# Output projection: its weights and first operands made beside the last segment's projections, in tiles taken over from them

## The chip, the cores and the metric

One core of one Trainium2 chip. The metric is the device time of one execution in microseconds (us). The engines are PE (TensorE, matmuls), DVE (VectorE), ACT (ScalarE), POOL (GpSimd) and SP (SyncE, which issues most DMAs); each runs its own instructions in order.

## What is computed

A transformer block on x of 2048 rows and 512 columns, in fp32. The reference, cut to what matters:

```python
mod = (silu(c) @ w_mod).reshape(1, 6, 1, 512)          # sa, ca, ga, sb, cb, gb
h = layernorm(x) * (1 + ca) + sa
# attention in N = 4 segments of 512 rows, 32 heads of 16
q, k, v = h @ wq, h @ wk, h @ wv
for s in range(4):
    p = softmax(q_s k_s^T / 4 + mask)                  # mask: -1e9 where query index < key index
    a_mem = phi(q_s) M / (phi(q_s) z + 1e-6)
    o_s = g * a_mem + (1 - g) * (p @ v_s)
    M, z = M + phi(k_s)^T v_s, z + sum(phi(k_s))
x = x + ga * (o @ wo)                                  # the output projection
h = layernorm(x) * (1 + cb) + sb
x = x + gb * (((h @ w_gate) * (h @ w_up)) @ w_down)    # 1376 features
```

## The kernel before, in words

**fp32 by three products.** An operand a of the projections is kept as a high part aH (fp32r, a copy by ACT) and a low part aL = a - aH (a subtraction by DVE or POOL). A product is then three matmuls: high x high, low x high, high x low.

**Stages.** At the start, the modulation and the projections of segment 0. Then the attention loop (line 1088), passes v from -2 to 32, for 32 units u of four heads each (eight units a segment). Pass v, in five slots, makes the maxima of units v+1 and v+2 (`q_step`: logits on PE, masked maximum on DVE), the exponentials of unit v (`k_step`: logits on PE, Exp on ACT, masking on POOL), and the sums p @ v of unit v-1 (`av_step`, slot 1: 32 matmuls into "tb", line 353). Behind the loop come the rest of segment 3's output projection and the GLU (lines 1272 to 1451).

**Work beside the attention.** Other PE work is written as generators that yield a cost after each small group of matmuls. In each slot `fill` (line 1019) adds a quarter of the rate (5.2 from pass 20 on, so 1.3 a slot; slot 1 adds nothing) to a credit and takes steps of the generators until the credit is used: first `fill_a`, and when that has ended `fill_b`. A step that yields 0.0 takes no credit, `False` ends the slot, and `None` says that nothing can be done yet. `weave(a, b, at)` takes steps of b behind those steps of a whose number stands in `at`. `pin` orders an instruction behind the PE instruction issued last.

- `fill_a` (line 932): K and Q projections of the four head groups of each segment (`a_kq`: 12 matmuls into "kps" or "qps", a yield of 0.68 after each three), V (`a_v`), the layer norm of the next segment, the memory sums (`a_mem`, `a_memT`). In the last segment, s = 3, it goes K, Q of group 0, V, K, Q of groups 1 and 2, then Q and K of group 3. Behind V it loads the attention output of segment 0 (`wo_load`, tiles "orl") and the first two of four row blocks of wo (`wo_raw`, tiles "wor"), which POOL scales by ga (line 916).
- `fill_b` (line 988): `open_b` closes the projections' pool `pa` and opens `bc` and `pb` in its place, allocates the output projection's weights woH and woL there, loads and scales row blocks 2 and 3 of wo, and splits all four into woH (ACT, line 928) and woL (POOL and DVE, line 929). Beside it `wo_op(0)` splits the operands of segment 0 into oH (ACT, line 487) and oL (DVE, line 490, in place). The first four of these steps yield `False`, one a slot (`paced`). Then `wo_mm(0)`: for each of four row tiles t, four steps of three matmuls into "wops" (line 517), a yield of 0.68 after each, and then `wo_add`, which adds x (tile "xr", loaded by `xr_load`) on DVE and stores the row tile. Woven into it are the rest of the operands, the first tile of the GLU's weights (`prep`, lines 432 to 449) and the operands of segment 1. Segments 1 and 2 follow, with the layer norms `lnC`.

**Pools.** `wpool` lasts for the whole kernel. `pa` holds the projections' tiles, `pb` the output projection's, `pc` the GLU's. With `reuse_waits="tile"` a tile in a new pool waits for the old tiles that lay in its place. A tag with n buffers hands them round; each new tile waits for the readers of the n-th before it.

Of the kernel before, what the change touches and what calls it, by code (L numbers as in the profile page):

```python
# [58 lines left out]
def tile_kernel(ctx, tc, x, wq, wk_, wv, wo, beta, w_gate, w_up, w_down, c, w_mod, out):  # L59
# [414 lines left out]

    def wo_op(s, pb, rw, us, gs=range(NG)):

        for g in gs:
            oH = pb.tile([P, L], F32R, tag="oH", name=f"oH{s}_{g}", bufs=8)
            if last(s * NG + g):
                a = bank(f"op{s}_{g}")  # L480
                for t in range(4):
                    TP(a[:, t * P:(t + 1) * P], orows[s * NG + g][:, t * P:(t + 1) * P], ident)
                oL = pb.tile([P, L], F32R, tag="oH", name=f"oL{s}_{g}", bufs=8)
            else:
                a = rw[g]
                oL = a.bitcast(F32R)
            act.activation(oH, a, AF.Copy)
# [13 lines left out]
        for _ in a:  # L501
            yield False

    def xr_load(s, pb):
        xrs = []
        for t in range(4):
            xr = pb.tile([P, D], F32, tag="xr", name=f"xr{s}_{t}", bufs=4)
            pin(nc.sync.dma_start(xr, x[rows(s, t), :]))
            xrs.append(xr)
        return xrs  # L510

    def wo_row(ps, t, us, gs, late=False):
        woH, woL = B["wo"]
        for i in gs:
            o = [(us[i][0], woH), (us[i][1], woH), (us[i][0], woL)]
            for j, (a, b) in enumerate(o[::2] + o[1:2] if late else o):
                MM(ps, a[:, t * P:(t + 1) * P], b[:, i, :], start=i == 0 and j == 0, stop=i == NG - 1 and j == 2)
            yield 0.68

    def wo_add(s, t, xr, ps):  # L520
        pin(vec.tensor_add(xr, xr, ps))
        nc.sync.dma_start(x1d[s][t], xr)

    def wo_mm(s, us, pb):

        xrs = xr_load(s, pb)
        for t in range(4):
            ps = bank(f"wops{s}_{t}")
            yield from wo_row(ps, t, us, range(NG))
            wo_add(s, t, xrs[t], ps)  # L530

    def lnC(s, pool, hpool, xpool, tag, nb):
        xt = []
# [152 lines left out]
    def load_g(nm, w, g):  # L686

        A, V = (CA if g == 0 else act), (CV if g == 0 and nm == "q" else nc.gpsimd)
        raw = staged(f"{nm}{g}")
        hi = wH[nm, g] = pa.tile([P, KT, P], F32R, name=f"w{nm}H{g}", bufs=1)  # L690
        lo = wL[nm, g] = pa.tile([P, KT, P], F32R, name=f"w{nm}L{g}", bufs=1)
        pin(nc.sync.dma_start(raw.rearrange("p (k c) -> p k c", c=P),
                              w.rearrange("(k p) n -> p k n", p=P)[:, :, g * P:(g + 1) * P]))
        yield
        hi, lo = (a.rearrange("p k (d h) -> p k h d", h=HG) for a in (hi, lo))
        raw = raw.rearrange("p (k h d) -> p k h d", k=KT, h=HG)
        pin(A.activation(hi, raw, AF.Copy))
        V.tensor_sub(lo, raw, hi.bitcast(F32))
        yield

    def load_v():
        raws = []
        for k in range(KT):
            wH["v", k] = pa.tile([P, D], F32R, name=f"wvH{k}", bufs=1)
            wL["v", k] = pa.tile([P, D], F32R, name=f"wvL{k}", bufs=1)
# [204 lines left out]

    B = {"h0": []}

    def wo_raw(k, pool, tag, n):
        raw = pool.tile([P, D], F32, tag=tag, name=f"wor{k}", bufs=n)
        pin(nc.sync.dma_start(raw, wo[k * P:(k + 1) * P, :]))
        nc.gpsimd.tensor_mul(raw, raw, gab)
        return raw

    def open_b():
        close(papool)  # L920
        B["bcpool"], B["bc"] = open_pool(name="bc", bufs=1, side="right", reuse_waits="tile")
        B["pbpool"], B["pb"] = open_pool(name="pb", bufs=2, side="right", reuse_waits="tile")
        pb = B["pb"]
        B["wo"] = woH, woL = [pb.tile([P, KT, D], F32R, name=n, bufs=1) for n in ("woH", "woL")]
        raws = B["raw"] + [wo_raw(k, pb, "x1", 4) for k in (2, 3)]
        yield
        for k in range(KT):
            pin(act.activation(woH[:, k, :], raws[k], AF.Copy))
            (vec if k % 2 else nc.gpsimd).tensor_sub(woL[:, k, :], raws[k], woH[:, k, :].bitcast(F32))
            yield  # L930

    def fill_a():
        for w in w2:
            next(w)
        yield from av
        memq.extend((a_mem(0, 0), a_mem(0, 1)))
        lns = None
        for s in range(NSEG):
            if s > 0:
                hcur[0] = yield from lns  # L940
                if s < 3:
                    r = load_mod(2 * s)
            for g in range(2 if s == 0 else 0, NG):
                ws = []
                if s == 0 and g < 3:
                    ws = [load_g(nm, w, g + 1) for nm, w in (("k", wk_), ("q", wq))]
                for w in ws:
                    next(w)
                K, Q = a_kq(s, g, "k"), a_kq(s, g, "q")
                if g >= 2 and s + 1 < NSEG:  # L950
                    if g == 2:
                        xts[s + 1] = xload(s + 1)
                        lns = a_ln(s + 1)
                        Q = weave(Q, lns, (0, 1, 2, 3) if s > 0 else (2, 3))
# [12 lines left out]
                for w in ws:  # L967
                    next(w)
                yield from Q
                if s > 0 and g == 0:  # L970
                    while vfree[0] < s:
                        yield None
                    if s < 3:
                        yield from weave(a_v(s), mod_acc(r), (1, 3, 5, 7))
                        yield from a_mod(2 * s, r[0])
                        r = load_mod(2 * s + 1)
                    else:
                        yield from a_v(s)
                        B["orl"] = wo_load(0, wpool)
                        B["raw"] = [wo_raw(k, wpool, "wor", 2) for k in (0, 1)]  # L980
                if g == 1 and 0 < s < 3:
                    yield from a_mod(2 * s + 1, r[0])
                memq.append(a_mem(s, g))
        while memq or memt:
            yield mem_step() or 0.0
            yield False

    def fill_b():
        ob = open_b()
        next(ob)  # L990
# [17 lines left out]
        yield from weave(wo_mm(2, us[2], pb), lg, (0, 1, 2, 3, 4, 5, 6, 7, 8, 9))  # L1008
        B["hf"] = yield from lg

    def kept_as(nm, g):
# [137 lines left out]
    NPT = 8  # L1149
# [57 lines left out]
    def product(q, i, j):  # L1207
# [276 lines left out]
```

## Time and profile before

| | us |
|---|---|
| median of three runs | 892.75 |
| lowest and highest | 890.75, 893.81 |
| the profiled execution, its own time | 888.0 |
| its span, first to last instruction | 886.3 |

Mean granted clock of PE over the span: 0.990 of full speed. A row of the timeline reads: start, length, engine, line, instruction, out<-in, shape, count, and in brackets the engine's idle time just before it with what ended it. A row of a tile's view reads: line, engine, instruction, out<-in, count, shortest/median/longest in ns, first and last start. L40 is a helper's line through which DVE and some ACT instructions are recorded, L90 and L93 those for matmuls and transposes.

### The profile page before, as it was taken

What the parts mean: (1) busy time and instruction counts of PE and PEld (TensorE: products, weight loads), DVE (VectorE), ACT (ScalarE), POOL (GpSimd) and SP (SyncE); (2) the same over time, 40 slices, a digit from 0 to 9 for tenths busy, and PEclk for the clock granted to TensorE, in tenths of its full rate; (3) what the DMA queues carried; (4) which work ended last, traced back from release to release, by engine and by line L of the source; (5) the groups of instructions that cost most, each with busy time, mean ns of one, the idle gap of its engine ahead of it and who ended that gap; (6) DMA issues with size and microseconds to landing.
All of it is one profiled execution on the core that took longest, in us unless ns stands there. A gap on an engine that the chain in (4) does not pass through costs nothing.

```text
span 886.3 us, 14413 instructions
## 1 busy us (share of the span) xinstructions
PE 835.0 (94%) x4823; PEld 583.0 (66%) x4824; DVE 656.0 (74%) x1728; ACT 472.8 (53%) x740; POOL 420.2 (47%) x564
## 2 busy tenths in 40 slices
PE   8998999989999989999789898999999999999998
PEld 5765565655565556655355566788778888887886
DVE  8597577986778868888878859898794856666532
ACT  3757667777676776667634664342363622333321
POOL 4545446546455755456533443887300746560000
PEclk9999899999999999999999999999999999999999
DMA  7674456665647665677875553543513341212032
GB/s 236 219 235 161 131 161 195 220 213 172 207 142 249 200 190 157 199 236 224 279 206 182 168 172 104 168 152 101 175 30 110 95 126 52 67 54 92 0 117 95
DMA packets 112667, 139.46 MB, mean 157 GB/s; under 512 B 20112, under 2 KB 71312, under 8 KB 112592
## 3 DMA queue, kind: packets, MB, share of 16 engines
q1 hardware_dynamic: 106368, 130.91, 47.6%
q10 hardware_dynamic: 6224, 7.62, 2.4%
q8 instruction: 38, 0.62, 0.3%
q14 instruction: 37, 0.30, 0.1%
HBM read 87.48 MB, written 50.76 MB: 156 GB/s over the span
## 4 chain that ended last, share of the span: by engine, by line
PE 67%; DVE 16%; ACT 5%; DMA 4%; issue 3%; POOL 3%; ACTq 1%; SPq 1%; DVEq 0%; POOLq 0%
PE g L90 22%; PE acc L90 14%; PE tb L90 7%; DVE q L40 6%; PE k L90 5%; PE q L90 5%; PE vps L90 4%; PE kps L90 2%; PE qps L90 2%; ACT pt L330 2%; PE wops L90 2%; POOL ahL L223 1%; DVE nm L40 1%; DMA xr<-in_x_dram 1%; PE up L90 1%
## 5 line engine op out<-in xcount | busy, mean ns | idle before, releaser
L40 DVE CUSTOM_DVE_ANT_0 q<-q,cmask 128x384 f32<-128x384 f32 (+3 forms) x512 | 246.6, 508 | 73.3 <-PE q L90 63.5
L330 ACT ACTIVATE pt<-k 128x1024 f32<-128x1024 f32 x160 | 163.9, 1024 | 70.3 <-PE k L90 56.8
L333 POOL TENSOR_SCALAR_AFFINE_SELECT pt<-pt 128x256 f32<-128x256 f32 (+1 forms) x224 | 102.2, 470 | 178.3 <-ACT pt L330 174.5
L90 PE MATMUL q<-kst,qst 96*128 96x384 bf16 (+3 forms) x512 | 102.3, 301 | 13.1 <-DVE nm L40 10.8
L90 PE MATMUL k<-qst,kst 98*128 98x384 bf16 (+3 forms) x512 | 97.5, 302 | 11.1 <-ACT pt L330 9.5
L448 POOL TENSOR_TENSOR w<-w 128x256 f32<-128x256 f32 (+1 forms) x84 | 70.7, 853 | 57.2 <-DMA w<-in_w_up_dram 38.2
L443 POOL TENSOR_TENSOR AL<-w,AH 128x512 fp32r<-128x512 f32 (+1 forms) x42 | 58.8, 1401 | 49.2 <-ACT AH L439 48.0
L90 PE MATMUL tb<-pt,v 128*32 128x512 f32 (+3 forms) x1024 | 80.3, 456 | 0.0
L90 PEld LDWEIGHTS <-kst 98*128 98x128 bf16 x512 | 38.6, 98 | 56.1 <-issue 47.2
L40 DVE DVE_READ_ACCUMULATOR2_ANT nm<- 128x1 f32 x512 | 72.3, 141 | 0.0
L90 PEld LDWEIGHTS <-qst 96*128 96x128 bf16 x512 | 43.6, 98 | 40.4 <-issue 14.5
L439 ACT ACTIVATE AH<-w 128x512 fp32r<-128x512 f32 (+3 forms) x88 | 46.8, 564 | 36.5 <-POOL w L448 21.3
L1426 DVE TENSOR_TENSOR mL<-mid,mH 128x512 fp32r<-128x512 f32 (+1 forms) x44 | 32.9, 752 | 41.4 <-ACT mH L1425 40.6
L90 PEld LDWEIGHTS tb<-pt,v 128*32 128x32 f32 x1024 | 29.8, 114 | 42.1 <-issue 38.4
L90 PE MATMUL acc<-DH,mL 128*128 128x512 f32 x144 | 56.6, 393 | 0.9 <-DVE mL L1426 0.9
L90 PE MATMUL acc<-DH,mH 128*128 128x512 f32 x144 | 57.1, 397 | 0.0
L90 PE MATMUL acc<-DL,mH 128*128 128x512 f32 x144 | 56.5, 392 | 0.0
L1425 ACT ACTIVATE mH<-mid 128x512 fp32r<-128x512 f32 (+1 forms) x44 | 27.1, 627 | 51.7 <-PE acc L90 50.4
L1221 ACT ACTIVATE p<-g 128x512 f32<-128x512 f32 (+1 forms) x22 | 13.1, 596 | 74.7 <-PE g L90 74.7
L443 DVE TENSOR_TENSOR AL<-w,AH 128x512 fp32r<-128x512 f32 (+3 forms) x44 | 30.5, 702 | 18.1 <-ACT AH L439 17.1
L359 ACT ACTIVATE tsb<-tb 128x512 f32<-128x512 f32 x32 | 19.1, 596 | 40.9 <-PE tb L90 40.9
L90 PE MATMUL g<-t_0H,AH 128*128 128x512 f32 (+1 forms) x88 | 34.7, 394 | 1.9 <-DVE u L1230 1.8
(286 smaller groups left out, 2062.4 us busy)
## 6 DMA issues: line engine op xcount, KB each, us to landing
kst<-kd SPq DMA_DIRECT2D x32, 384.0 KB
qst<-qd SPq DMA_DIRECT2D x32, 384.0 KB
td<-tsb ACTq DMA_DIRECT2D x28, 256.0 KB
wm<-in_w_mod_dram SPq DMA_DIRECT2D x24, 256.0 KB
kd<-k SPq DMA_DIRECT2D x16, 384.0 KB
qd<-q SPq DMA_DIRECT2D x16, 384.0 KB
w<-in_w_gate_dram SPq DMA_DIRECT2D x40, 128.0 KB
w<-in_w_up_dram SPq DMA_DIRECT2D x40, 128.0 KB
```

The lines of the kernel that those rows point to most:

```text
L40: i = getattr(self.eng, name)(*a, **k)
L90: return pe(nc.tensor.matmul(*a, **k))
L223: nc.gpsimd.tensor_sub(lo, h, hi.bitcast(F32))
L330: lpt[0] = act.activation(pt, kp, AF.Exp, scale=0.25)
L333: sels[u, i] = nc.gpsimd.affine_select(w, w, pattern=[[0, w.shape[1]], [1, P]], compare_op=ALU.is_ge, fill=0.0, base=0, channel_multiplier=-1)
L359: act.activation(tsbs[u], tbs.pop(u), AF.Copy)
L439: i = act.activation(hi[sl], w[sl], AF.Copy)
L443: i = eng.tensor_sub(lo[sl], w[sl], hi[sl].bitcast(F32))
L448: i = ce.tensor_tensor(w[:, o, :, 0:n], w[:, x, :, 0:n], w[:, y, :, 0:n], op=op)
L1221: lcp[0] = act.activation(r["p1"], ps, AF.Copy)
L1425: pin(act.activation(mH[0:n], md[0:n], AF.Copy))
L1426: vec.tensor_sub(mL[0:n], md[0:n], mH[0:n].bitcast(F32))
```

## The change

- The projections' weights of group 0 (wkH0, wkL0, wqH0, wqL0) and of V (8 tiles) move from `pa` to `wpool`, under the tags "four" (4 buffers) and "eight" (8 buffers).
- The output projection's weights become eight tiles of tag "eight": they take over those of V, which V of segment 3 reads last. Segment 0's four high operands take over "four", read last by K and Q of group 0 in segment 3. Later takers of "four" are one operand of segment 1, the four of segment 2 and the last two of segment 3, then the GLU's middle tiles 0 to 3; "eight" goes on to the GLU's temporaries, which had 8 buffers in `pc`. The tag "oH" in `pb` has 4 buffers in place of 8.
- Scaling and splitting wo, now `wo_weights`, and `wo_op(0)` become one chain of 18 steps that take no credit. It is woven into K and Q of groups 1 and 2 and Q of group 3 of the last segment. Row blocks 0 and 1 of wo are loaded at its start, 2 and 3 into the same two "wor" tiles after the first two are split.
- The first two row tiles of segment 0's output projection run at the end of `fill_a`, behind K of group 3, with x in two tiles of `pa`'s tag "x". `fill_b` begins with the other two row tiles; segment 1's operands are woven into them from the fourth step on, and the first tile of the GLU's weights moves into segment 1's row tiles. `paced` and `both` are no longer called.

```diff
     def wo_op(s, pb, rw, us, gs=range(NG)):
+        def half(nm):
+            if s % 2 == 0 or g == NG - 1:
+                return wpool.tile([P, L], F32R, tag="four", name=nm, bufs=4)
+            return pb.tile([P, L], F32R, tag="oH", name=nm, bufs=4)
         for g in gs:
-            oH = pb.tile([P, L], F32R, tag="oH", name=f"oH{s}_{g}", bufs=8)
+            oH = half(f"oH{s}_{g}")
...
-                MM(ps, a[:, t * P:(t + 1) * P], b[:, i, :], start=i == 0 and j == 0, stop=i == NG - 1 and j == 2)
+                MM(ps, a[:, t * P:(t + 1) * P], b[i], start=i == 0 and j == 0, stop=i == NG - 1 and j == 2)
...
-    def wo_mm(s, us, pb):
-        xrs = xr_load(s, pb)
-        for t in range(4):
+    def wo_mm(s, us, xrs, ts=range(4)):
+        for t, xr in zip(ts, xrs):
...
+    us = [[], [], []]
+    def wo_weights():
+        raw = {}
+        def raw_load(k):
+            raw[k] = wpool.tile([P, D], F32, tag="wor", name=f"wor{k}", bufs=2)
+            pin(nc.sync.dma_start(raw[k], wo[k * P:(k + 1) * P, :]))
+        def scaled(k):
+            pin(nc.gpsimd.tensor_mul(raw[k], raw[k], gab))
+        def halves(k):
+            hi, lo = (wpool.tile([P, D], F32R, tag="eight", name=f"wo{c}{k}", bufs=8) for c in "HL")
+            pin(act.activation(hi, raw[k], AF.Copy))
+            (vec if k % 2 else nc.gpsimd).tensor_sub(lo, raw[k], hi.bitcast(F32))
+            for o, x in zip(B["wo"], (hi, lo)):
+                o.append(x)
+        B["wo"] = [], []
+        raw_load(0)
+        raw_load(1)
+        for f, k in ((None, 0), (scaled, 0), (halves, 0), (scaled, 1), (halves, 1), (raw_load, 2), (raw_load, 3),
+                     (scaled, 2), (halves, 2), (scaled, 3), (halves, 3)):
+            if f is not None:
+                f(k)
+            if f != raw_load or k == 3:
+                yield 0.0
...
     def fill_a():
...
+                if s == NSEG - 1 and g == 1:
+                    xr0 = xr_load(0, pa, (0, 1), "x")
+                    ready = chain(wo_weights(), wo_op(0, None, B["orl"], us[0]))
+                if s == NSEG - 1 and 0 < g < NG - 1:
+                    K, Q = weave(K, ready, (0, 1, 2, 3)), weave(Q, ready, (0, 1, 2, 3))
                 if s == NSEG - 1 and g == NG - 1:
-                    yield from Q
+                    yield from weave(Q, ready, (0, 1, 2, 3))
                     memq.append(a_mem(s, g))
                     yield from K
+                    yield from ready
+                    yield from wo_mm(0, us[0], xr0, (0, 1))
                     break
...
                         B["orl"] = wo_load(0, wpool)
-                        B["raw"] = [wo_raw(k, wpool, "wor", 2) for k in (0, 1)]
...
     def fill_b():
-        ob = open_b()
-        next(ob)
+        open_b()
         pb, bc = B["pb"], B["bc"]
+        rest = wo_mm(0, us[0], xr_load(0, pb, (2, 3)), (2, 3))
         o1 = wo_load(1, pb)
         pr = prep(0, "0_0", bc, 1, pb, 1)
         next(pr)
-        us = [[], [], []]
-        first = both(wo_op(0, pb, B["orl"], us[0]), ob)
-        yield from paced(islice(first, 4))
-        yield from weave(wo_mm(0, us[0], pb), chain(first, both(chain(iter((0.0,) * 4), pr), wo_op(1, pb, o1, us[1]))),
-                         (0, 0, 1, 2, 4, 5, 6, 7, 9, 10, 12, 13))
+        yield from weave(rest, wo_op(1, pb, o1, us[1]), (3, 4, 4, 5, 5, 6, 6, 7))
         B["o0"] = True
         lg = lnC(0, pb, bc, pb, "x1", 4)
-        yield from weave(wo_mm(1, us[1], pb), islice(lg, 10), (1, 5, 6, 7, 8, 9, 11, 12, 13, 14))
+        yield from weave(wo_mm(1, us[1], xr_load(1, pb)), chain(pr, islice(lg, 10)), (0, 1, 2, 3, 4, 6, 7, 8, 9, 10, 11, 12, 13, 14))
...
-        return pc.tile([P, L], dt, tag="pt", name=name, bufs=NPT)
+        return wpool.tile([P, L], dt, tag="eight", name=name, bufs=8)
...
-            m0 = pc.tile([P, L], F32, tag="mid0", name=f"mid0_{q}_{i}", bufs=NF)
+            if i < 4:
+                m0 = wpool.tile([P, L], F32, tag="four", name=f"mid0_{q}_{i}", bufs=4)
+            else:
+                m0 = pc.tile([P, L], F32, tag="mid0", name=f"mid0_{q}_{i}", bufs=NF - 4)
```

More of the change, by code (lines that the diff above doesn't have):

```diff
@@ L482, in wo_op @@
                     TP(a[:, t * P:(t + 1) * P], orows[s * NG + g][:, t * P:(t + 1) * P], ident)
-                oL = pb.tile([P, L], F32R, tag="oH", name=f"oL{s}_{g}", bufs=8)
+                oL = half(f"oL{s}_{g}")
             else:
@@ L502, in paced, with xr_load @@
             yield False
-    def xr_load(s, pb):
+    def xr_load(s, pb, ts=range(4), tag="xr"):
         xrs = []
-        for t in range(4):
-            xr = pb.tile([P, D], F32, tag="xr", name=f"xr{s}_{t}", bufs=4)
+        for t in ts:
+            xr = pb.tile([P, D], F32, tag=tag, name=f"xr{s}_{t}", bufs=4)
             pin(nc.sync.dma_start(xr, x[rows(s, t), :]))
@@ L522, in wo_add @@
         nc.sync.dma_start(x1d[s][t], xr)
-    def wo_mm(s, us, pb):
-        xrs = xr_load(s, pb)
-        for t in range(4):
+    def wo_mm(s, us, xrs, ts=range(4)):
+        for t, xr in zip(ts, xrs):
             ps = bank(f"wops{s}_{t}")
             yield from wo_row(ps, t, us, range(NG))
-            wo_add(s, t, xrs[t], ps)
+            wo_add(s, t, xr, ps)
     def lnC(s, pool, hpool, xpool, tag, nb):
@@ L689, in load_g @@
         raw = staged(f"{nm}{g}")
-        hi = wH[nm, g] = pa.tile([P, KT, P], F32R, name=f"w{nm}H{g}", bufs=1)
-        lo = wL[nm, g] = pa.tile([P, KT, P], F32R, name=f"w{nm}L{g}", bufs=1)
+        if g == 0:
+            hi, lo = (wpool.tile([P, KT, P], F32R, tag="four", name=f"w{nm}{c}0", bufs=4) for c in "HL")
+        else:
+            hi, lo = (pa.tile([P, KT, P], F32R, name=f"w{nm}{c}{g}", bufs=1) for c in "HL")
+        wH[nm, g], wL[nm, g] = hi, lo
         pin(nc.sync.dma_start(raw.rearrange("p (k c) -> p k c", c=P),
@@ L703, in load_v @@
         for k in range(KT):
-            wH["v", k] = pa.tile([P, D], F32R, name=f"wvH{k}", bufs=1)
-            wL["v", k] = pa.tile([P, D], F32R, name=f"wvL{k}", bufs=1)
+            wH["v", k] = wpool.tile([P, D], F32R, tag="eight", name=f"wvH{k}", bufs=8)
+            wL["v", k] = wpool.tile([P, D], F32R, tag="eight", name=f"wvL{k}", bufs=8)
             raws.append(staged(f"v{k}"))
@@ L911, in tile_kernel @@
     B = {"h0": []}
[L913 to L917, printed above, removed]
+    us = [[], [], []]
[21 more added lines that the diff above has]
+                yield 0.0
     def open_b():
@@ L922, in open_b @@
         B["pbpool"], B["pb"] = open_pool(name="pb", bufs=2, side="right", reuse_waits="tile")
[L923 to L930, printed above, removed]
     def fill_a():
@@ L1007, in fill_b @@
         lg = lnC(1, pb, bc, pb, "x1", 4)
-        yield from weave(wo_mm(2, us[2], pb), lg, (0, 1, 2, 3, 4, 5, 6, 7, 8, 9))
+        yield from weave(wo_mm(2, us[2], xr_load(2, pb)), lg, (0, 1, 2, 3, 4, 5, 6, 7, 8, 9))
         B["hf"] = yield from lg
@@ L1236, in product @@
         elif j == 4:
-            m0 = pc.tile([P, L], F32, tag="mid0", name=f"mid0_{q}_{i}", bufs=NF)
+            if i < 4:
+                m0 = wpool.tile([P, L], F32, tag="four", name=f"mid0_{q}_{i}", bufs=4)
+            else:
+                m0 = pc.tile([P, L], F32, tag="mid0", name=f"mid0_{q}_{i}", bufs=NF - 4)
             vec.tensor_add(r["p1"], ps, r["p1"])
```

1 line of the change is left out of this document (removed).

## The prediction

> **What bounds the kernel now.** I read the page first, for the engine that fills the span and the engines on the chain that ended last.
>
> ```profile
> span 886.3 us, 14413 instructions
> PE 835.0 (94%) x4823; PEld 583.0 (66%) x4824; DVE 656.0 (74%) x1728; ACT 472.8 (53%) x740; POOL 420.2 (47%) x564
> PE 67%; DVE 16%; ACT 5%; DMA 4%; issue 3%; POOL 3%; ACTq 1%; SPq 1%; DVEq 0%; POOLq 0%
> ```
>
> TensorE (PE) is busy for 94% of the span and makes two thirds of the chain. The change moves matmuls and adds none, so it can only win time in which PE waits or runs at a reduced clock: 886.3 - 835.0 = 51.3 us of waiting in all, of which the part near the change has to be found. For that I cut the attention loop into its passes. Every pass v issues one group of 32 "tb" matmuls (line 353) in its second slot, so the stretch from one tb group to the next is one pass long; I name it by the pass it begins in. The view by windows gives, behind the bounds, the length, the busy time of PE, PEld, DVE, ACT and POOL, the granted clock, the DMA share and GB/s.
>
> ```profile
> 364.81:377.14 12.33, 12.33 (x93) 7.58 (x92) 10.90 (x39) 8.22 (x12) 7.12 (x11) 1.00 0.51 156
> 377.14:391.10 13.96, 12.98 (x92) 7.76 (x91) 11.48 (x39) 10.52 (x15) 8.75 (x13) 1.00 0.73 243
> 391.10:404.30 13.20, 12.97 (x97) 8.35 (x96) 10.81 (x39) 9.24 (x15) 7.75 (x12) 1.00 0.60 191
> 404.30:418.03 13.73, 11.86 (x90) 7.28 (x89) 11.22 (x40) 9.75 (x16) 8.46 (x12) 1.00 0.82 254
> 418.03:429.69 11.66, 9.60 (x74) 4.88 (x73) 9.71 (x39) 9.24 (x15) 7.15 (x11) 0.95 0.80 254
> 429.69:455.57 25.88, 19.17 (x109) 11.31 (x108) 19.82 (x49) 12.72 (x20) 14.84 (x19) 0.96 0.78 231
> 455.57:469.97 14.40, 14.40 (x90) 8.34 (x89) 11.01 (x42) 5.25 (x6) 2.57 (x6) 0.88 0.80 238
> ```
>
> The first four rows are ordinary passes (21 to 24, the last segment's projections): 12.3 to 14.0 us each, PE idle for 0.98, 0.23 and 1.87 us in three of them, 3.08 us together. Then comes the **hole**: pass 25 has PE idle for 2.06 us, pass 26 lasts 25.88 us with 6.71 us idle, and pass 27 is full but at a clock of 0.88. The three take 51.94 us. The same windows for the tile wops, the output projection's sums, show what PE got done there.
>
> ```profile
> 418.03:429.69 11.66, 0.00 (x0) 0.00 (x0) 0.00 (x0) 0.95 0.80 254
> 429.69:455.57 25.88, 11.13 (x42) 7.58 (x42) 1.88 (x3) 0.96 0.78 231
> 455.57:469.97 14.40, 6.71 (x24) 4.36 (x24) 1.44 (x3) 0.88 0.80 238
> ```
>
> Sixty-six output matmuls: none in pass 25, where the projections are over and the output projection's operands do not exist yet, 42 in pass 26, 24 in pass 27. PE's timeline says what it waited for, and how fast it ran.
>
> ```profile
> 418.03 2.36 PE L90 MATMUL tb<-pt,v 128*32 128x512 f32 x32
> 420.32 0.73 PE L90 MATMUL up<-MZ,phq 128*128 128x136 f32 x4
> 421.76 0.60 PE L93 MATMUL mT<-ident,mem 128*128 128x128 f32 x4
> 436.62 0.60 PE L90 MATMUL k<-qst,kst 98*128 98x384 bf16 x4 [2.51 <-ACT pt L330]
> 441.16 0.50 PE L90 MATMUL wops<-woH,orl 128*128 128x512 f32 x1 [1.55 <-DVE orl L40]
> 442.67 0.40 PE L90 MATMUL wops<-woH,orl 128*128 128x512 f32 x1
> ...
> 444.98 0.39 PE L90 MATMUL wops<-woL,oH 128*128 128x512 f32 x1
> ...
> 454.35 0.38 PE L90 MATMUL q<-kst,qst 96*128 96x256 bf16 x2 [1.66 <-DVE nm L40]
> ...
> 455.57 4.05 PE L90 MATMUL tb<-pt,v 128*32 128x512 f32 x32
> ```
>
> The waits trace back to making the operands (line 487, line 490, lines 928 and 929) in the middle of the loop: ACT and DVE do that work ahead of the attention's exponentials and maxima, and PE stands. The same 32 tb matmuls take 2.36 us at 418.03 and 4.05 us at 455.57, just after two such waits: that is the price of the clock.
>
> **The change part by part.** First, *the room to win*. Pass 27 holds 24 output matmuls in 14.40 us without a wait; less the 4.05 - 2.36 = 1.69 us of its slow tb group it is 12.71 us. One output matmul is (444.98 - 442.67)/10 = 0.231 us from start to start. After the change the first two row blocks of segment 0 (24 matmuls, 8 steps of 0.68 credit) stand directly behind the last projection, ahead of the switch to the second generator. At 1.3 credit a slot, 5.2 a pass, I count 6 steps for pass 25 (the memory steps take some credit there) and 8 each for 26 and 27: 66 matmuls, the same stand at 469.97 as now, at 22 a pass. A pass of 22 costs 12.71 - 2 x 0.231 = 12.25 us; three cost 36.75, and the 0.73 + 0.60 us of the "up" and "mT" matmuls that pass 25 has besides make 38.1. Against 51.94 that leaves **13.9 us**.
>
> *What ordinary passes lose anyway*: 3.08 us in four, so 2.3 us in three. That stays.
>
> *What moves into passes 21 to 23.* The 18 steps of making operands ride on the projections' steps of groups 1 and 2 and the first of group 3, where they take no credit. Their prices stand in the views of the tiles wor and oH.
>
> ```profile
> L916 POOL TENSOR_TENSOR wor<-wor,gab x4: 1268/1278/1282, 366.0 to 432.9; 128x512 f32<-128x512 f32 x4
> L928 ACT ACTIVATE woH<-wor x4: 614/619/624, 428.1 to 437.0; 128x512 fp32r<-128x512 f32 x4
> L929 POOL TENSOR_TENSOR woL<-wor,woH x2: 1263/1266/1268, 428.8 to 434.7; 128x512 fp32r<-128x512 f32 x2
> L40 DVE TENSOR_TENSOR woL<-wor,woH x2: 677/684/691, 430.5 to 437.6; 128x512 fp32r<-128x512 f32 x2
> ```
> ```profile
> L487 ACT ACTIVATE oH<-orl x14: 618/626/638, 427.6 to 525.3; 128x512 fp32r<-128x512 f32 x14
> L40 DVE TENSOR_TENSOR orl<-orl,oH x14: 679/693/1795, 428.8 to 525.9; 128x512 fp32r<-128x512 f32 x14
> ```
>
> ACT gets 4 x 0.62 + 4 x 0.63 = 5.0 us more in three passes where it is busy 27.98 of 39.49: hidden. POOL gets two more scalings and two subtractions, 4 x 1.27 = 5.1 us, on 23.62: hidden, as far as POOL itself goes. DVE gets 2 x 0.68 + 4 x 0.69 = 4.1 us, and there the cover is thin: it is busy 33.19 of 39.49 us, so 6.30 us are free, and its free time is time in which it waits for PE's next q. I take half of the 4.1 us as absorbed there and 2.1 us as lengthening the passes; the ends are 0 (all of it fits into 6.30) and 4.1 (none does).
>
> ```profile
> 366.01 2.51 POOL L916 TENSOR_TENSOR wor<-wor,gab 128x512 f32<-128x512 f32 x2
> ```
> ```profile
> 367.35 1.19 DVE L40 TENSOR_TENSOR nh<-nm,nh 128x16 bf16<-128x16 f32 x1
> 379.21 0.18 DVE L40 TENSOR_TENSOR nh<-nm,nh 128x16 bf16<-128x16 f32 x1
> 428.83 1.79 DVE L40 TENSOR_TENSOR orl<-orl,oH 128x512 fp32r<-128x512 f32 x1
> ```
> ```profile
> 428.81 1.27 POOL L929 TENSOR_TENSOR woL<-wor,woH 128x512 fp32r<-128x512 f32 x1 [0.42 <-ACT woH L928]
> ```
>
> These rows show a second price: a DVE subtraction of 16 columns takes 0.18 us alone and 1.19 us while POOL's scaling of 366.01 to 368.52 runs, and an operand subtraction 1.79 us instead of 0.69 beside POOL's at 428.81. The four POOL instructions that come newly into these passes can do this again, at up to 1.0 us each: 0 to 4. I take 0 for it beyond the half above, because today's two scalings lie in pass 21, which PE still ran through without a gap. The Trainium skill (SBUF — State Buffer, Who interferes with whom) says that a DVE instruction with two inputs from SBUF and a GpSimd instruction that reads SBUF exclude one another for the whole instruction, whoever issues first. By that rule all six moved subtractions can be held up, which speaks against the change; the rows agree with it, and its outcome is the third rival.
>
> *Added waits.* The raw rows 2 and 3 take the two "wor" tiles over from rows 0 and 1, so their loads stand on SP's queue until POOL and DVE have read those tiles, with the K and Q stores and the loads of later passes behind them. Those loads run up to three passes ahead, so a wait of one POOL instruction (1.27 us) is covered: 0, at most 1.3. POOL's scaling of row 2 follows its load by one step.
>
> ```profile
> POOL wor L916 <- DMA wor<-in_wo_dram: 1.6, 1, 1.6
> ```
>
> Today POOL waited 1.6 us in that place; behind it stand the masks and the "kr" differences for which ACT waits. I take 0.4 us, from 0 to 1.6 twice. So passes 21 to 23 grow by 2.1 + 0.4 = **2.5 us** (0 to 8).
>
> *The switch.* Opening the second generator still issues ten transfers at once: two x tiles, segment 1's four operands, and the first weight tile. Today's rows show what such a burst costs.
>
> ```profile
> 427.97 1.85 SPq L471 DMA_DIRECT2D orl<-od  x4
> ...
> 437.20 2.95 SPq L508 DMA_DIRECT2D xr<-in_x_dram  x4
> ```
> ```profile
> 433.50 0.63 ACT L487 ACTIVATE oH<-orl 128x512 fp32r<-128x512 f32 x1 [1.79 <-DMA orl<-od]
> ```
> ```profile
> 445.08 0.69 DVE L40 TENSOR_TENSOR xr<-xr,wops 128x512 f32<-128x512 f32 x1 [3.37 <-DMA xr<-in_x_dram]
> ```
>
> From issue to use it took 5.5 us for the operands (ACT waited 1.79) and 7.9 us for x (DVE waited 3.37). After the change the x tiles go first, and the first use of either comes three to four steps later, half a pass or some 6 us. So most of it is covered; I take **2.0 us**, between 0 and 1.79 + 3.37 = 5.2.
>
> *The first weight tile's split* (lines 439 to 448) slips from pass 26 into 27 and 28. POOL is busy 2.57 of 14.40 us there and ACT 5.25, so I take 0.5 us; for DVE's two instructions in it, at the 0.69 of line 490, at most 1.4. *The renamed buffers* ("eight", "four") keep their numbers: 8 for the GLU's temporaries, 4 + 7 for the 11 middle tiles, and each earlier user ends in the projections or the output projection, long before. Zero; if one were late, a wait of one DVE instruction, 0.7 us.
>
> **Sum**: 13.9 - 2.3 - 2.5 - 2.0 - 0.5 = 6.6 us gained. The profiled execution's own time is 888.0 us, 4.75 below the median of the runs, so it would come to 881.4, and the median of 892.75 to **886.2**.
>
> **The rivals.** (1) *Everything hides*: DVE absorbs its 4.1 us and the burst is covered. Then 13.9 - 2.3 = 11.6 us are gained: 881.2. For it: PE ran without a gap through pass 21 with two scalings in it; against it: DVE at 84% and ACT and DVE waits at every switch.
>
> (2) *The burst takes the place of the hole*: the new second half of segment 0 finds x and segment 1's operands as late as now, so the pass of the switch loses 3.37 + 1.79 + 2.51 and another slow tb group, 9.4 us in place of 2.0. The gain is 6.6 - 7.4 = -0.8: 893.5, no change that can be told. For it: the same ten transfers at the same place; against it: two x loads and two weight loads fewer in the burst, and a later first use.
>
> (3) *DVE becomes the bound of passes 21 to 23.* Each of the six moved subtractions waits for a POOL instruction (1.79 us each, 10.7) and the four new POOL instructions hold up another of DVE's at 1.0 us, 4.0; DVE's 6.30 us of waiting for q stay, since each q needs the maximum before it. The passes grow by 14.7 and the gain left is 13.9 - 2.3 - 2.0 - 0.5 = 9.1: slower by 5.6, 898.4. It decides the sign from 9.1 us of growth on. For it: the 1.19 and 1.79 us rows; against it: they are the worst of their kind, and orl's median is 0.693.
>
> (4) *The change doesn't do what it says*: the operands are not ready when the last projection ends, so nothing fills pass 25. Against it: 18 steps on 20 places, all called before the last K. Then 892 to 894.
>
> **How the numbers follow.** Forecast 0.46, with its own range from 882.5 (growth and burst at half) to 890 (both near their upper middle); rival 1 0.16; rival 2 0.16; rival 3 0.17; rival 4 0.05. A measurement of this kernel can tell about 0.3%, 2.7 us, from no change. Faster by more than that: forecast, rival 1 and a part of 2, 0.70. Within: most of 2 and 4, 0.12. Slower: rival 3 and a little of 2, 0.18. The range for 8 in 10 takes in the forecast, rivals 1, 2 and 4 and the mild end of 3: 880.5 to 895.
>
> **What would show it.** Output matmuls right behind the last "kps", in the pass after it, and no tb group of 3 to 4 us; passes 25 to 27 at 13 to 14.5 us each. Woven operands: L916, L928 and L487 inside the last segment, and passes 21 to 23 longer by 1 to 4 us together; over 9 would make rival 3 right. At the switch, a wait of DVE on xr or ACT on orl of 2 us; over 5 makes rival 2 right. The forecast is wrong if the passes behind 27 or the GLU change their length by over a microsecond, which I cost at nothing.

## The result, and the profile after

The changed kernel takes 881.42 us in the median of four runs (880.14 to 881.91), the one before 891.75 in four runs beside it (886.2 to 893.81). The ratio of the means is 0.9892, with a 95% interval of 0.9845 to 0.9939: 5.4 to 13.8 us less. On another chip (a5_change, last experiments) the ratio was 0.9944 (0.9918 to 0.9969): 2.8 to 7.3 us less. The profiled execution took 881.91 us in all; its page begins:

```profile
span 879.8 us, 14406 instructions
PE 832.8 (95%) x4824; PEld 583.0 (66%) x4824; DVE 650.6 (74%) x1728; ACT 472.5 (54%) x740; POOL 424.1 (48%) x564
```

The same cut into passes 21 to 29, from tb group to tb group (length, busy time of PE, PEld, DVE, ACT, POOL, granted clock, DMA share, GB/s):

```profile
363.14:375.51 12.37, 12.37 (x92) 7.58 (x91) 9.49 (x38) 9.87 (x16) 6.90 (x11) 1.00 0.64 187
375.51:390.18 14.67, 13.25 (x91) 7.87 (x90) 13.73 (x41) 12.20 (x18) 13.75 (x15) 1.00 0.81 259
390.18:403.68 13.50, 13.08 (x97) 8.30 (x96) 11.67 (x43) 8.84 (x15) 9.64 (x14) 1.00 0.67 211
403.68:417.86 14.18, 12.16 (x90) 7.24 (x89) 11.81 (x41) 10.07 (x16) 8.68 (x13) 1.00 0.76 238
417.86:430.78 12.92, 12.92 (x97) 8.05 (x96) 11.04 (x40) 7.67 (x11) 6.12 (x10) 1.00 0.64 192
430.78:443.01 12.23, 12.18 (x88) 7.30 (x87) 10.00 (x38) 5.22 (x6) 4.71 (x8) 1.00 0.70 224
443.01:461.27 18.26, 13.26 (x90) 7.92 (x89) 14.19 (x45) 9.93 (x15) 9.39 (x13) 1.00 0.96 306
461.27:477.99 16.72, 13.70 (x90) 7.97 (x90) 13.08 (x46) 8.08 (x12) 5.58 (x13) 1.00 0.68 199
477.99:494.86 16.87, 13.31 (x92) 8.00 (x92) 14.51 (x47) 10.67 (x15) 6.30 (x11) 0.90 0.38 119
```

The output projection's matmuls (tile wops) in passes 24 to 27:

```profile
403.68:417.86 14.18, 0.85 (x3) 0.56 (x3) 0.00 (x0) 1.00 0.76 238
417.86:430.78 12.92, 5.26 (x18) 3.16 (x18) 0.68 (x1) 1.00 0.64 192
430.78:443.01 12.23, 6.03 (x21) 3.80 (x21) 0.99 (x2) 1.00 0.70 224
443.01:461.27 18.26, 6.76 (x24) 4.29 (x24) 1.58 (x3) 1.00 0.96 306
```

Passes 25 and 26 are full, at full clock, and take 25.15 us where they took 37.54. The same 66 output matmuls are done at the end of pass 27. But pass 27 has 5.00 us of idle PE and takes 18.26 us, not 14.40, and 28 and 29 take 33.59 us, not 30.89. Passes 21 to 24 take 54.72 us, not 53.22. The whole difference of the spans, 6.5 us, adds up as in the table. Its last column sets a second profile of the change, from the other chip (a5_change), against the same profile of the kernel before; there the difference is 7.7 us.

| stretch | change, us | in a5_change |
|---|---|---|
| up to the tb group of pass 21 (364.81 to 363.14) | -1.67 | -0.35 |
| passes 21 to 24 | +1.50 | +2.40 |
| passes 25 and 26 | -12.39 | -12.38 |
| passes 27 to 29 | +6.56 | +3.67 |
| passes 30 and 31 | +0.29 | -0.23 |
| from the last tb group to the end (362.96 to 362.17) | -0.79 | -0.81 |

So of what the hole gave up, half was taken back at once in the first profile, and 0.3 of it in the second. PE's timeline shows where in pass 27:

```profile
447.65 0.59 PE L90 MATMUL k<-qst,kst 98*128 98x512 bf16 x2 [2.28 <-ACT pt L330]
...
457.38 0.60 PE L90 MATMUL k<-qst,kst 98*128 98x256 bf16 x4 [2.26 <-ACT pt L330]
...
460.30 0.60 PE L90 MATMUL k<-qst,kst 98*128 98x512 bf16 x2 [0.43 <-DMA qst<-nt]
```

PE waits for an exponential (pt) twice, for 2.28 and 2.26 us, and then 0.43 us for the transfer of a qst tile. ACT's timeline shows what stood ahead of the two exponentials: copies that waited for segment 1's operands, then a DMA issue for the next unit's qst tile.

```profile
444.79 0.63 ACT L492 ACTIVATE oH<-orl 128x512 fp32r<-128x512 f32 x1 [3.36 <-DMA orl<-od]
...
454.31 1.90 ACTq L310 DMA_DIRECT2D qst<-nt  x2
456.31 1.02 ACT L330 ACTIVATE pt<-k 128x1024 f32<-128x1024 f32 x1 [4.50 <-DVE nm L40]
```

The last row names DVE's nm as what ended ACT's idle time. That the DMA issue held this exponential is read from the order alone: the issue ended at 456.21, just before it. What the issue itself waited for is not shown.

SP's timeline and waits show why the operands came late. Its load of x waited 3.6 us for the store of the second row tile (issued at 435.91), and the four operand loads stand behind it:

```profile
435.91 0.34 SPq L527 DMA_DIRECT2D x1d<-xr  x1
439.91 0.81 SPq L513 DMA_DIRECT2D xr<-in_x_dram  x2
440.78 1.84 SPq L471 DMA_DIRECT2D orl<-od  x4
```
```profile
SPq L513 <- DMA x1d<-xr: 4.0, 2, 3.6
```

### The profile page after: what moved, and what is told of

Its sections match the earlier page's. It is cut to its first block, busy times and chain, and to the rows that moved or that the text cites. A ratio compares the mean times of both kernels' runs of the same rounds, so it can differ in the third digit from the quotient of the medians.

```text
span 879.8 us, 14406 instructions
## 1 busy us (share of the span) xinstructions
PE 832.8 (95%) x4824; PEld 583.0 (66%) x4824; DVE 650.6 (74%) x1728; ACT 472.5 (54%) x740; POOL 424.1 (48%) x564
## 4 chain that ended last, share of the span: by engine, by line
PE 66%; DVE 13%; DMA 8%; ACT 5%; POOL 4%; issue 3%; ACTq 1%; SPq 0%; POOLq 0%; DVEq 0%
PE g L90 23%; PE acc L90 14%; PE tb L90 5%; DVE q L40 5%; PE k L90 5%; PE q L90 5%; PE vps L90 4%; PE kps L90 3%; PE qps L90 2%; ACT pt L330 2%; DMA xr<-in_x_dram 2%; PE wops L90 2%; POOL ahL L223 1%; DVE x L40 1%; DVE nm L40 1%
## 5 line engine op out<-in xcount | busy, mean ns | idle before, releaser
L333 POOL TENSOR_SCALAR_AFFINE_SELECT pt<-pt 128x256 f32<-128x256 f32 (+1 forms) x224 | 105.4, 484 | 174.3 <-ACT pt L330 173.9
L90 PE MATMUL tb<-pt,v 128*32 128x512 f32 (+3 forms) x1024 | 76.2, 438 | 0.2 <-POOL pt L333 0.2
L90 PEld LDWEIGHTS <-qst 96*128 96x128 bf16 x512 | 43.6, 98 | 39.1 <-issue 14.4
L439 ACT ACTIVATE AH<-w 128x512 fp32r<-128x512 f32 (+3 forms) x88 | 46.8, 565 | 33.6 <-POOL w L448 20.5
L90 PE MATMUL g<-chH,AH 128*128 128x512 f32 (+1 forms) x88 | 34.8, 395 | 0.7 <-ACT p L1245 0.7
```

What stands on the lines that cost most here:

```text
L90: return pe(nc.tensor.matmul(*a, **k))
L333: sels[u, i] = nc.gpsimd.affine_select(w, w, pattern=[[0, w.shape[1]], [1, P]], compare_op=ALU.is_ge, fill=0.0, base=0, channel_multiplier=-1)
L439: i = act.activation(hi[sl], w[sl], AF.Copy)
```

## The experiments

The theory: the gain is passes 25 and 26, filled because the operands exist, and the loss behind it is the switch, whose transfers now all fall into pass 27. The rivals: the moved tiles alone do it; the two early row tiles do it, by covering the switch; the loss is an order of ACT's copies and not the burst. Pass lengths are a fine instrument where nothing moves: passes 7 and 9 to 12 of all fourteen profiles agree within 0.1 us. A pass in which the granted clock drops is 0.4 to 3 us longer (pass 17 took 16.9 us at 0.90 and 16.5 at 1.00, pass 24 16.7 at 0.80 and 13.4 to 14.4 at 1.00), so each is read with its clock. And some passes spread at full clock too: pass 22 took 14.67 us in one profile of the change and 15.57 in the other. By the end of pass 27 every version has done the same 66 output matmuls.

**Tiles alone** (r1_tiles). The change's tiles, with the steps where they were:

```diff
-                    ready = chain(wo_weights(), wo_op(0, None, B["orl"], us[0]))
...
-                    K, Q = weave(K, ready, (0, 1, 2, 3)), weave(Q, ready, (0, 1, 2, 3))
...
-                    yield from ready
-                    yield from wo_mm(0, us[0], xr0, (0, 1))
...
+                        B["ob"] = wo_weights()
+                        for _ in range(3):
+                            next(B["ob"])
...
+        ob = B["ob"]
...
+        first = both(wo_op(0, pb, B["orl"], us[0]), ob)
+        yield from paced(islice(first, 4))
```

As in the kernel before, the first two row blocks of the weights are loaded and scaled behind V of segment 3, and everything else is done behind the group loop.

> The tiles of the change (four, eight, oH of 4 buffers) with the old times: wo's first two row blocks scaled behind V, everything else of the output projection behind the switch, the first four steps paced. Theory (the gain comes from filling pass 25 and from having the operands before pass 26): passes 25 and 26 together stay near 37.5 us as before, the time stays at 889 to 894. Rival (the renamed tiles alone free the switch): passes 25 and 26 fall below 33 us and the time comes under 887.

Measured: 889.93 us against 886.62 of the kernel before on that chip, ratio 1.0039 (1.0014 to 1.0064). Its passes 25 and 26:

```profile
414.28:425.63 11.35, 9.21 (x74) 4.79 (x73) 9.35 (x39) 9.15 (x13) 7.47 (x11) 1.00 0.77 245
425.63:456.77 31.14, 22.27 (x109) 13.49 (x108) 19.89 (x49) 11.32 (x17) 16.23 (x18) 0.84 0.63 201
```

The hole is there, 42.49 us, 5 us wider than before, though part of that is a clock of 0.84. With two wor tiles for four row blocks the second pair cannot be loaded until the first is split, and the output sums waited 3.5 us once for woH. The tiles alone gain nothing in the loop; they only make room for the early steps. They do have the shorter end, though (362.08 us behind the last tb group, against 362.96 before), so that part of the table is the tiles'.

**Early operands, no early rows** (r2_norows).

```diff
-                    xr0 = xr_load(0, pa, (0, 1), "x")
...
-                    yield from wo_mm(0, us[0], xr0, (0, 1))
...
-        rest = wo_mm(0, us[0], xr_load(0, pb, (2, 3)), (2, 3))
+        rest = wo_mm(0, us[0], xr_load(0, pb), range(4))
...
-        yield from weave(rest, wo_op(1, pb, o1, us[1]), (3, 4, 4, 5, 5, 6, 6, 7))
+        yield from weave(rest, wo_op(1, pb, o1, us[1]), (11, 12, 12, 13, 13, 14, 14, 15))
```

> Operands and weights early as in the change, but all four row tiles of segment 0 behind the switch. If the early operands are the gain and the place of the rows is secondary, passes 25 to 28 come to 57 to 61 us, near the 60.1 of the change, and the time to 880 to 884. If the two row tiles ahead of the switch are what covers its transfers, pass 25 keeps 2 us or more of idle PE, x arrives late, and the time comes to 884 to 889.

Measured: 878.25 us, ratio 0.9904 (0.9871 to 0.9937). Passes 25 to 28:

```profile
419.02:435.17 16.15, 14.96 (x96) 9.58 (x95) 9.62 (x39) 7.56 (x11) 6.11 (x10) 0.89 0.82 266
435.17:447.73 12.56, 12.33 (x88) 7.30 (x87) 10.58 (x39) 7.44 (x10) 4.72 (x8) 1.00 0.92 284
447.73:461.47 13.74, 13.25 (x91) 7.83 (x90) 12.96 (x43) 8.35 (x12) 9.98 (x13) 1.00 0.90 289
461.47:476.11 14.64, 13.41 (x91) 7.82 (x90) 13.59 (x47) 7.88 (x11) 5.33 (x13) 1.00 0.62 184
```

Passes 25 to 28 take 57.09 us, where the change takes 60.13 (59.17 in its second profile), although the clock was at 0.89 in 25; pass 24, at the same clock, took 15.42 us, 1.2 more than in the change. The early operands are the gain. The switch comes one pass earlier (x loads issued at 427.30, not 439.91), its x loads do not wait for a store from a tile of the pool that goes, and segment 1's operands are first used twelve steps after their load, not four. The early rows are not needed as a cover; they push everything else of the switch into pass 27.

**x in the wor tiles** (r3_wor).

```diff
-                    xr0 = xr_load(0, pa, (0, 1), "x")
...
+                    xr0 = xr_load(0, wpool, (0, 1), "wor", 2)
```

The load stands behind the last split of the weights, ahead of K of group 3.

> The change with the first two x tiles in the two wor tiles of the lasting pool instead of two tiles of the projections' pool. Theory: the 3.6 us that SP waited at the switch for the store of the second row tile came from the new pool lying over that x tile; then the ten transfers are issued about 3.6 us earlier, ACT's 3.4 us wait for segment 1's operands shrinks below 1, and pass 27 falls from 18.3 to 14.5 to 16.5 us, the time to 878 to 880. Rival (the burst itself is the bound, DMA busy 0.96 in that pass): pass 27 stays within 1 us of 18.3.

Measured: 879.01 us, ratio 0.9925 (0.9900 to 0.9950). Passes 26 and 27, and what SP's load of the operands waited for:

```profile
433.18:447.06 13.88, 12.32 (x87) 7.36 (x86) 10.93 (x40) 6.75 (x10) 4.76 (x8) 1.00 0.92 294
447.06:462.03 14.97, 13.20 (x91) 7.87 (x90) 13.36 (x44) 8.45 (x13) 9.72 (x13) 1.00 0.87 268
```
```profile
SPq L471 <- DMA rb<-rdd: 2.3, 1, 2.3
```

Half right. The wait for the store is gone from the x loads and pass 27 falls into the forecast 14.5 to 16.5, but the operand loads now wait 2.3 us for another transfer, and pass 26 is 1.65 us longer. The two together are 28.85, where the change has 30.49 and 29.97 in its two profiles: 1.1 to 1.6 us, not 3.

**Pinned copies** (r4_pin, and once more r10_pin). A pinned instruction is held behind the last matmul written ahead of it.

```diff
-            act.activation(oH, a, AF.Copy)
+            pin(act.activation(oH, a, AF.Copy))
```

> The change with ACT's copies into oH held behind the PE instruction issued last, as DVE's subtractions are. Theory: the copies of segment 2's operands were drawn forward into pass 28, where ACT waited 1.2 and 2.4 us for their loads and PE 1.35 us for the exponentials behind them; then pass 28 falls from 16.7 to about 15.2 and the time by 1 to 2 us, to 879 to 880.5. Rival (copies at a later place only move the wait): passes 28 and 29 together stay at 33.6 within 0.7.

Measured: 878.26 us, ratio 0.9897 (0.9868 to 0.9925). Pass 28 took 15.10 us, and 15.44 in r10_pin; the change took 16.72 in its profile and 16.28 in a second one (a5_change). In the change three of segment 2's four copies run at 460.77 to 465.89, and two of them wait for their load ahead of the exponentials:

```profile
460.77 0.63 ACT L492 ACTIVATE oH<-orl 128x512 fp32r<-128x512 f32 x1 [1.18 <-DMA orl<-od]
462.21 0.62 ACT L492 ACTIVATE oH<-orl 128x512 fp32r<-128x512 f32 x1
465.26 0.63 ACT L492 ACTIVATE oH<-orl 128x512 fp32r<-128x512 f32 x1 [2.43 <-DMA orl<-od]
```

In r10_pin the four of them run from 485.11, in pass 29, without a wait for a load:

```profile
485.11 0.63 ACT L492 ACTIVATE oH<-orl 128x512 fp32r<-128x512 f32 x1 [0.80 <-DVE nm L40]
487.36 0.62 ACT L492 ACTIVATE oH<-orl 128x512 fp32r<-128x512 f32 x1
490.49 1.15 ACT L492 ACTIVATE oH<-orl 128x512 fp32r<-128x512 f32 x2
```

So the copies drawn forward are one cause of pass 28's excess. That the pin gains anything over the passes together is not shown, since pass 27 is longer with it (granted clocks other than 1.00 in brackets):

| | pass 27 | pass 28 | pass 29 | together |
|---|---|---|---|---|
| the change | 18.26 | 16.72 | 16.87 (0.90) | 51.85 |
| the change, a5_change | 17.73 (0.90) | 16.28 | 14.95 | 48.96 |
| pinned, r4_pin | 18.88 (0.91) | 15.10 | 15.62 | 49.60 |
| pinned, r10_pin | 18.95 (0.91) | 15.44 | 15.22 | 49.61 |

The 33.6 us for passes 28 and 29 against which the rival was set rest on a pass 29 at a clock of 0.90; the second profile has 31.23, and the pinned ones 30.72 and 30.66.

**Weight tile loaded later** (r5_lateW, on the pinned version).

```diff
-        next(pr)
...
-        yield from weave(wo_mm(1, us[1], xr_load(1, pb)), chain(pr, islice(lg, 10)), (0, 1, 2, 3, 4, 6, 7, 8, 9, 10, 11, 12, 13, 14))
+        yield from weave(wo_mm(1, us[1], xr_load(1, pb)), chain(pr, islice(lg, 10)), (0, 2, 3, 4, 5, 6, 7, 7, 8, 9, 10, 11, 12, 13, 14))
```

> The change with the pinned copies, and with the four loads of the GLU's first weight tile moved from the switch into the first step of segment 1's row tiles, half a megabyte out of the burst. Theory (pass 27 is long because the transfers at the switch fill the DMA engines, 0.96 busy): pass 27 falls from 18.9 us of the pinned version to 16.5 to 17.5, passes 28 and 29 stay at 15.1 and 15.6 within 0.5, the time at 876 to 877.5. Rival (the pass waits for the order of the loads, segment 1's operands behind the x tiles, and not for their sum): pass 27 stays within 0.5 of 18.9.

Measured: 882.23 us, ratio 0.9934 (0.9911 to 0.9956), which neither reading had expected. Passes 27 and 28, and the first of the moved loads:

```profile
444.20:462.22 18.02, 14.87 (x91) 8.84 (x90) 12.15 (x42) 8.48 (x12) 3.96 (x8) 0.91 0.95 292
462.22:481.07 18.85, 13.72 (x90) 7.82 (x89) 14.68 (x49) 8.31 (x12) 9.53 (x20) 1.00 0.64 194
```
```profile
455.43 1.35 SPq L432 DMA_DIRECT2D w<-in_w_gate_dram  x2
```

Half a megabyte less at the switch took 0.9 us from pass 27, and pass 28, where most of the weight tile's split now lies, is 3.4 to 3.75 us longer than in the pinned version. But the moved loads were issued from 455.43 on and so still fall into pass 27, whose DMA share stays at 0.95. The run therefore does not tell the sum of the bytes from their order, and which of them makes pass 27 long stays open.

**Both** (r6_pin_norows, and r11_pin_norows): the edits of r2_norows and r4_pin.

> Early operands, all four row tiles behind the switch, and the pinned copies. The kernel without early rows took 15.42, 16.15, 12.56, 13.74, 14.64, 15.36 us for passes 24 to 29, the pinned one gained in passes 28 and 29. If both gains add up: 28 and 29 together 29.3 to 30.0 and the time 876.5 to 878; if the pin only mends what the late switch of the change made: no difference to 878.25 by more than 0.7.

Measured: 877.53 us, ratio 0.9877 (0.9825 to 0.9928). Passes 28 and 29 take 14.88 + 15.63 = 30.51 us, not under 30.0, and without the pin they took 14.64 + 15.36: where the operands come in time, the pin has nothing to mend. The better median lies within the runs' spread.

**Scaling left out** (r7_noscale).

```diff
-            pin(nc.gpsimd.tensor_mul(raw[k], raw[k], gab))
+            pass
```

> The change without POOL's four scalings of wo by ga (this part of the computation is left out). It tells what made passes 21 to 24 longer by 1.5 us (54.72 against 53.22). If POOL's instructions hold DVE's up, 5.1 us of POOL fewer bring the four passes to 53.2 to 54.0; if DVE's own added subtractions are the price, they stay at 54.4 to 55.

One execution took 880.85 us. Passes 22 to 24 took 15.73, 13.22 and 16.74 us, the last of them so:

```profile
403.46:420.20 16.74, 15.16 (x89) 8.99 (x88) 12.12 (x41) 10.17 (x16) 8.66 (x13) 0.80 0.66 212
```

Inconclusive. Pass 23 is back at its old 13.2 us, but pass 22 is 1.1 us longer than in the change's first profile, and pass 24 ran at a clock of 0.80. Passes 22 and 23 together, 28.95 us, lie between the 28.17 and 29.06 of the change's two profiles.

**DVE doubled** (r8_dve2).

```diff
             pin(vec.tensor_sub(oL, a, oH.bitcast(F32)))
+            if s == 0:
+                pin(vec.tensor_tensor(oL, a, a, op=ALU.max))
```

> The change with a second DVE instruction of the same shape behind each of the four subtractions of segment 0's operands (4 x 0.69 = 2.8 us of DVE more in passes 22 to 24). If DVE's free time is mostly usable, the four passes grow by under 0.7 us; if half of it is (the forecast's share), by 1.4; if none, by 2.8.

Measured: 880.11 us in one execution. Passes 21 to 24 take 12.32 + 14.51 + 16.51 + 14.40 = 57.74 us, 3.0 more than the change's 54.72 (2.1 more than the 55.62 of a5_change). Pass 23, which got most of it, and the four added instructions:

```profile
387.58:404.09 16.51, 13.82 (x96) 8.30 (x95) 15.99 (x45) 10.65 (x17) 11.86 (x15) 1.00 0.68 220
```
```profile
L40 DVE TENSOR_TENSOR orl<-orl x4: 1003/1216/1535, 388.2 to 405.1; 128x512 fp32r<-128x512 f32 x4
```

DVE is busy for 15.99 of 16.51 us there, and PE waits 2.0 us for its maxima (nm): DVE bounds that pass. But the added instructions took 1.0 to 1.5 us each, 5.0 together, and not the 2.8 that the expectation counts. The change's own six subtractions took 6.1 and 5.7 us in its two profiles and cost 1.5 and 2.4; a further 5.0 cost 2.1 to 3.0. So more DVE work here has a price, of about half its length, and what is added first costs rather less; that the free time is used up is not shown.

**One chip for all.** Four versions beside 18 runs of the kernel before (median 887.83).

> The change itself once more, beside the three versions below on one chip, since medians of different chips differ by a few us. Expected: faster than before by 0.7 to 1.1%, passes 27 to 29 at 49 to 52 us together against 45.3 before, passes 25 and 26 at 25.2 against 37.5.

> Pinned copies and the first two x tiles in the wor tiles. If the store of the second row tile was what held the switch up and the pin mends pass 28: pass 26 at 13 to 14, 27 at 14.5 to 15.5, 28 at 15.1, the time 1 to 2 us under the pinned version. If the wait for the store only hid a wait for the other transfers: passes 26 and 27 together within 0.7 us of the 30.4 to 31.1 of the change and of the pinned version, and the same time.

> The pinned version again: 1 to 2.5 us under the change, all of it in passes 28 and 29.

> Early operands, all rows behind the switch, pinned: the switch lies in passes 24 to 26 at a cost of 1.7 us each in 25 and 26, passes 27 and 28 at 13.7 and 14.9. Expected 2 to 4 us under the change; if the early rows cover the switch after all, within 1 us of the pinned version or above it.

| | median us (lowest to highest) | ratio to before, 95% interval |
|---|---|---|
| the change (a5_change) | 884.41 (877.46 to 886.26) | 0.9944 (0.9918 to 0.9969) |
| pinned (r10_pin) | 880.80 (877.91 to 886.07) | 0.9927 (0.9899 to 0.9955) |
| pinned, x in wor (r9_pin_wor: both edits) | 879.37 (876.79 to 884.70) | 0.9908 (0.9876 to 0.9939) |
| pinned, no early rows (r11_pin_norows) | 877.88 (875.74 to 879.75) | 0.9883 (0.9858 to 0.9908) |

The change gained 0.56%, less than the 0.7 to 1.1% expected of it here. In r9_pin_wor passes 26 and 27 take 13.74 and 14.54 us, 2.2 and 1.7 less than the 30.49 and 29.97 of the change's profiles. But pass 28 is back at 16.52 with the copies pinned, and there PE waits 1.9 us for DVE's maxima, so the copies are not the only cause of a long pass 28. The last version, the early operands without the early rows, is the only one whose interval lies clear of the change's; its median is 6.5 us under it, where 2 to 4 were expected, and the pinned version's interval overlaps both. Its passes 25 to 28:

```profile
419.24:433.85 14.61, 13.42 (x96) 8.49 (x95) 9.89 (x40) 7.57 (x11) 6.27 (x10) 1.00 0.84 259
433.85:447.87 14.02, 12.33 (x88) 7.30 (x87) 11.26 (x40) 6.56 (x9) 4.22 (x8) 1.00 0.99 309
447.87:461.61 13.74, 13.23 (x91) 7.82 (x90) 12.54 (x42) 8.81 (x13) 9.95 (x13) 1.00 0.88 270
461.61:476.35 14.74, 13.41 (x90) 7.81 (x90) 13.67 (x47) 6.68 (x9) 5.42 (x13) 1.00 0.64 192
```

It too moves 309 GB/s through a whole pass of the switch, yet PE idles there for 1.69 us and not for 5. By GB/s times length, passes 25 to 28 move some 14 to 15 MB in either version, but at most 4.3 MB fall into one pass here, and 5.6 into pass 27 of the change: the transfers are spread out as well as early.

## Why the prediction was right, step by step

**The room** was right. 66 matmuls at the same stand, 12.92 and 12.23 us for passes 25 and 26 (forecast 12.25 + 1.33 and 12.25), tb groups of 2.36 us, a clock of 1.00 throughout. Passes 25 to 27 gave 51.94 - 43.41 = 8.5 us, where the terms 13.9 - 2.3 - 2.0 - 0.5 made 9.1. That the early operands fill the hole is shown: the tiles alone leave it (r1_tiles), and the early operands without the early rows fill it as well (r2_norows).

**The switch** was under-sized: 2.0 forecast, 5.0 us of idle PE in pass 27 measured, near the upper end of 5.2 (3.0 in a5_change, at a clock of 0.90). The step that failed is "the first use of either comes three to four steps later, half a pass or some 6 us". It counts from the switch, but the loads were issued only 4 us behind the store of the second row tile. ACT turned to the first operand at 441.43, 0.65 us after the issue of its load began, and got it 4.0 us after. One of the two waits of 2.3 us in pass 27 is traced to this; the other stands behind the qst issue, and its cause is open. The second rival, for which a wait of over 5 us was to speak, came close: ACT waited 4.0 us for segment 1's operands. The 0.5 us for the first weight tile cannot be told apart in pass 27. The 2.3 us of ordinary idle time in passes 25 to 27 did not appear beside it (0.05 us in 25 and 26), and that made up for most of the miss by luck.

**Passes 21 to 23** grew by 1.05 us (1.96 in a5_change), and 24 by 0.45, where 2.5 were forecast for 21 to 23. Most of it is pass 22, where DVE became tight (13.73 of 14.67 us). More DVE work has a price there, as r8_dve2 shows, and a part of the third rival acts too. Three of the six moved subtractions took 0.63 to 0.69 us, the others up to 1.65, and the longest began while POOL was in an instruction:

```profile
L40 DVE TENSOR_TENSOR orl<-orl,oH x14: 629/693/1654, 389.7 to 520.2; 128x512 fp32r<-128x512 f32 x14
```
```profile
403.58 1.65 DVE L40 TENSOR_TENSOR orl<-orl,oH 128x512 fp32r<-128x512 f32 x1
```
```profile
403.26 1.42 POOL L780 TENSOR_TENSOR q<-qr,q 128x512 bf16<-128x512 f32 x1
```

It ended 0.55 us after POOL's did, as if it had waited for the end of it. The rule that the prediction cited beside this rival (the Trainium skill, SBUF — State Buffer, Who interferes with whom) agrees with the trace that far. How much of the growth is the lock and how much the plain work stays open, since r7_noscale told nothing.

**The passes behind 27** were costed at nothing, and that failed by the prediction's own sign of over a microsecond: 28 and 29 grew by 2.7 us. In a5_change it was only 0.34: pass 28 grew by 1.2 us, and pass 29, which ran at a clock of 0.90 in the first profile, took 14.95 us at 1.00, less than before. In pass 28 one cause is the unpinned copies, drawn forward into a time when their loads had not landed; the rest is open.

**The ends** were costed at nothing too, and gave 2.5 us (1.2 in a5_change). The end behind the loop is the tiles' (362.1 us in r1_tiles, 362.2 in the change), where PE's wait for DVE in the first GLU tiles fell:

```profile
PE g L90 <- DVE u L1230: 1.8, 1, 1.8
```
```profile
PE g L90 <- DVE u L1251: 0.3, 1, 0.3
```

(The first row is of the kernel before, the second, the longest wait for DVE that is left, of the change.) Most of the start's part is pass 2, 14.71 us before and 13.34 after, by the clock. That this is chance is likely but not shown, with one profile of the kernel before.

So the forecast of 6.6 us met 6.1 in the profiled executions (888.0 to 881.91), and the ratios of both chips hold it; the medians differ by 10.3 us on the first chip and by 3.4 on the other. The mechanism, the filled hole, was right. That the sum came so close is in part luck: the 2.7 us lost behind pass 27 and the 2.5 us gained at the ends, both costed at nothing, cancel.

## What to carry to other kernels

Making operands while other work still fills the matmul engine was the gain here; moving the matmuls that use them forward as well added nothing that shows, and the version without it (r11_pin_norows) is the only one of four on one chip whose interval is clear of the change's. Where a pool is closed and its place reused, look at the last store out of it: the first load into its place stands behind that store, and everything behind that load on the queue with it. And a copy that nothing holds in its place may be drawn forward on an in-order engine until it waits for its load ahead of more urgent work. Holding it where its result is due took 0.8 to 1.6 us from one pass here, without a gain that can be told over the passes together.

## What the runs showed of the hardware

Much of the spread of a kernel's runs goes with the granted clock of PE. On one chip the change took 877.46 us at a mean clock of 0.997, 881.03 at 0.992 and 886.26 at 0.983; the kernel before 882.82 at 0.994 and 892.91 at 0.984. One stretch, pass 2, in which no wait of PE shows in either profile, ran at 0.87 before and at 0.96 after (the first row takes in 0.1 us more than the pass):

```profile
93.60:108.40 14.80, 14.80 (x100) 8.70 (x103) 10.00 (x38) 9.75 (x16) 6.25 (x10) 0.87 0.28 94
```
```profile
93.39:106.73 13.34, 13.34 (x97) 8.21 (x96) 9.93 (x38) 9.67 (x16) 6.20 (x10) 0.96 0.32 105
```

So one profile's pass that is 0.4 to 3 us longer is read with its clock, before a cause is sought. On that chip the fastest version also had the narrowest spread: 875.74 to 879.75 us in six runs of the one without early rows, 877.46 to 886.26 in twelve of the change. With six runs that may be chance.
